# Cosine attention and a GELU feed-forward layer: the last 256 rows of w_in loaded in two column halves

## The chip, the core and the metric

The kernel runs on one core of one Trainium2 chip. The metric is the device time of one execution in microseconds (us), lower is better. The core has a matrix engine (TensorE, "PE" in the profile), a vector engine (VectorE, "DVE"), an activation engine (ScalarE, "ACT"), a general engine (GpSimd, "POOL") and a synchronising engine (SyncE, "SP") that issues most of the DMA transfers. "PEld" is TensorE's weight load, which runs beside its matmuls. SP, ACT and POOL issue DMA transfers; those of POOL can change the type on the way (here 32-bit floats in memory to bf16 on the chip).

## The reference

Eight batches of 12 heads of 448 rows by 64 go through attention with normalised queries and keys. The result, as 3584 rows of 768, goes through two matrix products with an exact GELU between them.

```python
q_n = q / (norm(q, axis=-1) + 1e-06)            # q, k, v: (8, 12, 448, 64)
k_n = k / (norm(k, axis=-1) + 1e-06)
scores = q_n @ k_n.T / tau                      # tau = 0.1
attn = exp(scores - max(scores))
attn = attn / (sum(attn) + 1e-09)
x = (attn @ v).transpose(0, 2, 1, 3).reshape(3584, 768)
h = x @ w_in                                    # w_in: (768, 2048)
g = 0.5 * h * (1 + erf(h / sqrt(2)))
out = g @ w_out                                 # w_out: (2048, 768)
```

## The kernel before

The order of the work is written out by hand; each engine runs its instructions in that order, and semaphores hold an instruction until what it needs is there.

Heads are worked on in groups of four (a "quad"): three groups to a batch, 24 in all, counted from 0. (The steps of `attention_first` are numbered by units: group 0 is units 0 and 1, group g is unit g + 1.) For a group, q and k are loaded by SP (`load_qk`, L122 to 132), squared (`square`, L156 on GpSimd), summed (`reduce`, L165 on VectorE), and turned into reciprocal norms: logarithm and exponential on ScalarE (`logs`, `roots`, L172, L178, L181), a small add on GpSimd (L190) and a reciprocal on VectorE (L192). `scale` (L208, GpSimd) multiplies by them and writes bf16. `transposes` turns the result, on TensorE with copies by VectorE (L225, L230) for the first four groups, and by a DMA transpose issued from SP (L220) afterwards. `scores` (L246) are matmuls, `exps` (L253) ScalarE; `sums` (L266, L275) and `values` (L289) are matmuls again, and `turned`, `inverted`, `spread` and `normalise` (L297 to L323, VectorE) make the finished columns of x.

The feed-forward layer runs batch by batch. `first(b)` (L647) forms h for one batch: sixteen blocks m of 128 columns of w_in, each the sum of six matmuls over the six row tiles kd of w_in (L659), followed by the GELU on ScalarE (L696). It takes row tiles 0 to 3 for the first blocks ("ahead", five for batch 0) and only then row tiles 4 and 5 for these blocks, since the last columns of x come last. At m = 8 of batch 0 TensorE also turns group 3. After m = 5 of batch 0 ScalarE computes the norms of groups 4 and 5. The second product (L352) is cut into single matmuls that are filled in between the attention work of the next batch. SP stores the results (L341).

`attention_first` (L407) writes out the order for batch 0 line by line. The weights are loaded there, between GpSimd's computing, by DMAs issued from GpSimd: `load_wi` (L381) brings 256 rows of w_in at a time, in two transfers (one for each of two sets of 128 rows, laid on 64 partitions each), so that load n holds row tiles 2n and 2n + 1, with all 2048 columns. Loads 0, 1 and 2 stand at L420, L453 and L493. `load_wo` (L387) brings a quarter of w_out, `load_v` (L137) the values. All of GpSimd's transfers are in one queue (q0 in the profile) and go in the order of issue; those of SP are in another (q1), and the same 16 DMA engines serve both. Every GpSimd transfer uses one of eight semaphores in turn, so the issue of one waits until the one eight places before it has landed. `upto(f, n)` (L396) calls the steps of `f` that are still to be done, up to n of them. `spin` (L402) is a matmul without use.

The step around the change is L493 to L524: third load of w_in, the scale of group 2 (q at L483, k at L499), then the squares of groups 3 and 4 (L514 to L525), a part of w_out (L526) and the values of batch 1 (L527).

Of the kernel before, what the change touches and what calls it, by code (L numbers as in the profile page):

```python
# [16 lines left out]
def kernel(  # L17
# [18 lines left out]
    B, H, S, D = q.shape  # L36
    C = S // D
    NQ = H // 4
    NG = B * NQ
    d_model = H * D  # L40
    d_ff = moe_w_in.shape[1]
# [49 lines left out]
    wi = wpool.tile([128, KD, d_ff], BF16, tag="wi")  # L91
# [21 lines left out]
    NU = len(units)  # L113
    groups = [[n] for n in range(NQ + 2)] + [[NQ + 2, NQ + 3], [2 * NQ + 1], [2 * NQ + 2]]
# [20 lines left out]
    NV = len(v_parts)  # L135
# [64 lines left out]
    def scale(u, parts=None):  # L200
        g, s0, s1 = units[u]
        n, j = place[u]
        rn = rn_t[n][:, j]
        if g not in qkb_t:
            qkb_t[g] = qkbp.tile([128, 2, C, 2, D], BF16, tag="qkb", name=f"qkb{g}")
        qkb, t = qkb_t[g], qk_t[g]
        for eng, i in parts or ((nc.gpsimd, 0), (nc.gpsimd, 1)):
            eng.tensor_tensor(  # L208
                qkb[:, i, :, s0:s1].rearrange("p c s d -> p s c d"), t[:, i, s0:s1],
                rn[:, i].to_broadcast([128, s1 - s0, C, D]), ALU.mult)  # L210
# [16 lines left out]
    def copies(u, i):  # L227
        g, s0, s1 = units[u]
        rows = slice(64 * s0, 64 * s1)
        nc.vector.tensor_copy(qkT_t[g][rows, i], tp_t.pop((u, i))[rows])  # L230
# [47 lines left out]
    def values(g, chunks=range(C), p=None):  # L278
        for c in chunks:
            if c == 0 and g < NQ:  # L280
                bank_t[g, 0] = ps_acc.tile([128, 512], F32, tag="o", name=f"o{g}_0")
                bank_t[g, 1] = mm_tile(f"o{g}_1")
            elif c == 0:
                o = pair(p, f"o{g}")
                bank_t[g, 0], bank_t[g, 1] = o[:, 0], o[:, 1]
            for s in range(2):
                for h in range(2):
                    rows, cols = slice(64 * h, 64 * (h + 1)), slice(64 * s, 64 * (s + 1))
                    nc.tensor.matmul(bank_t[g, h][cols, :S], lhsT=v_t[g][rows, s, c, :],  # L289
                                     rhs=pt_t[g, s, c][rows], start=(c == 0), stop=(c == C - 1),  # L290
                                     tile_position=(64 * h, 64 * s))
# [86 lines left out]
        return [lambda c0=c0, c1=c1: part(c0, c1) for c0, c1 in ((0, 3 * n), (3 * n, 5 * n), (5 * n, 6 * n))]  # L378


    def load_wi(n):  # L381
        for s in range(2):
            nc.gpsimd.dma_start(
                out=wi[64 * s:64 * (s + 1), 2 * n:2 * n + 2, :],
                in_=moe_w_in.rearrange("(n s h d) f -> n s d h f", s=2, h=2, d=D)[n, s])

    def load_wo(i):  # L387
        n, c = KF // 2, slice(i // 2 * NH, (i // 2 + 1) * NH)
# [5 lines left out]
    done = {}  # L394

    def upto(f, n, last=None):  # L396
        last = {load_qk: NG, load_v: NV, root: len(groups), load_wi: NQ, load_wo: 4}.get(f, NU)
        while done.get(f, 0) < min(n, last):
            done[f] = done.get(f, 0) + 1
            f(done[f] - 1)  # L400
# [6 lines left out]
    def attention_first():  # L407
# [6 lines left out]
        reduce(0, K)  # L414
        square(1, ((AC, Q),))
        upto(load_v, 1)
        logs(0)
        reduce(1, Q)
        roots(0)
        upto(load_wi, 1)  # L420
        square(1, ((AC, K),))
        inverses(0)
# [17 lines left out]
        square(3, ((AC, K),))  # L440
        scale(1, ((GP, 1),))
        upto(load_qk, 5)
        spin(1)
        transposes(1, 0)
# [6 lines left out]
        scores(0, ((0, 2), (0, 3)))  # L451
        roots(2)
        upto(load_wi, 2)  # L453
        exps(0, ((0, 0), (0, 1)))
        inverses(2)
# [35 lines left out]
        exps(1, ((0, 0), (1, 0)))  # L491
        sums(0, (6,))
        upto(load_wi, 3)  # L493
        transposes(3, 0)
        turned(0)
        exps(1, ((0, 1), (1, 1)))
        scores(1, ((0, 2), (1, 2)))
        values(0, (0,))
        scale(3, ((GP, 1),))  # L499
        copies(3, 0)  # L500
        values(0, (1,))
        exps(1, ((0, 2), (1, 2)))
# [221 lines left out]
    for b in range(B):  # L724
        if b == 0:
            attention_first()
            acc.close()
            third.append(ctx.enter_context(tc.tile_pool(name="ps_third", bufs=1, space=bass.MemoryType.PSUM)))
        else:
            attention(b, fill)  # L730
        first(b)
        sb, hf = divmod(b, 2)
        todo = [(t, ni) for t in (range(3) if hf == 0 else range(3, 7)) for ni in range(2)]
        if b == 0:
            todo.sort(key=lambda x: x[1])
        tail = [2 * S // 128 - 1] if b == B - 1 else []
        fill = [f for t, ni in todo if t not in tail for f in second_pieces(sb, t, ni)]
        fill += [f for t in tail for f in last_pieces(sb, t)]
# [37 lines left out]
```

## Time and profile before

| | |
|---|---|
| median of 4 runs | 416.23 us (415.62 to 416.30) |
| the profiled execution, its own time | 417.82 us |
| its span, first to last instruction | 416.0 us |
| TensorE busy | 407.1 us (98%) |
| ScalarE busy | 248.8 us (60%) |
| VectorE busy | 188.1 us (45%) |
| GpSimd busy | 166.4 us (40%) |
| granted TensorE clock, mean | 0.996 |
| DMA: w_in, six transfers of 512 KB | 15.9 us median from issue to landing |

Times inside the profile are counted from the start of the span. A row of a timeline gives the start, the length (of all instructions merged into the row), the engine, the line, the operation, what is written and read, how many instructions, and in brackets the idle time of the engine just before and what ended it. Where an instruction waits for several things, the bracket names the one that came last. A granted clock of 1.00 is full speed and 0.50 is half. A row of the slices gives tenths in 40 slices of 10.4 us. Sizes of GpSimd's transfers are those written on the chip.

### The profile page before, as it was taken

The page shows a single profiled execution, that of the slowest core. Times are in us where ns is not written, and L with a number is a line of the kernel's source. Part 1 is how long each engine was busy: PE and PEld are TensorE (multiplying, and loading weights), DVE is VectorE, ACT ScalarE, POOL GpSimd, SP SyncE. Part 2 cuts the span into 40 slices and gives each one's busy share as a digit, 9 for nine tenths or more (in the row PEclk, how much of TensorE's full clock was granted, in tenths as well). Part 3 has the DMA queues.
Part 4 walks back from the last instruction along what each step waited for, and adds up shares of the span by engine and source line. Part 5 has one row for each costly group of instructions (what it writes and reads, how often), then busy time and mean ns, then how long its engine had stood idle before and what let it go on. Part 6 is the DMA issues. An engine that isn't in the chain of part 4 may idle for free.

```text
span 416.0 us, 8265 instructions
## 1 busy us (share of the span) xinstructions
PE 407.1 (98%) x3503; PEld 212.1 (51%) x3503; DVE 188.1 (45%) x379; ACT 248.8 (60%) x362; POOL 166.4 (40%) x113
## 2 busy tenths in 40 slices
PE   7997999999999999999999999999999999999996
PEld 3443555555555555555555555555555555555564
DVE  5786203943167322853148431683118711481021
ACT  6993677657745657745764548755655467754300
POOL 5998625066730719045540446318270243000000
PEclk9998999999999999999999999999999999999999
DMA  8999996834297314946197242975079130610033
GB/s 286 259 256 215 205 237 211 202 74 130 46 198 242 70 66 59 229 162 134 23 183 241 47 125 46 185 220 132 2 134 225 38 46 0 121 39 2 0 77 76
DMA packets 66196, 54.53 MB, mean 131 GB/s; under 512 B 38640, under 2 KB 62320, under 8 KB 66160
## 3 DMA queue, kind: packets, MB, share of 16 engines
q1 hardware_dynamic: 54464, 41.79, 39.2%
q0 software_dynamic: 11312, 11.80, 17.8%
q8 instruction: 27, 0.44, 0.5%
q10 hardware_dynamic: 384, 0.43, 0.3%
q14 instruction: 9, 0.07, 0.1%
HBM read 45.61 MB, written 11.01 MB: 136 GB/s over the span
## 4 chain that ended last, share of the span: by engine, by line
PE 90%; DMA 6%; ACT 1%; SPq 1%; POOL 0%; issue 0%; DVE 0%; DVEq 0%
PE op L352 35%; PE hp L659 35%; PE st L246 8%; PE o L289 7%; DMA wi<-in_moe_w_in_dram 4%; PE sm L275 4%; DMA qk<-in_k_dram 2%; PE op L371 1%; ACT pt L253 1%; SPq L129 1%; POOL qkb L208 0%; ACT sq L154 0%; PE tp L225 0%; ACT lq L172 0%; ACT root L178 0%
## 5 line engine op out<-in xcount | busy, mean ns | idle before, releaser
L253 ACT ACTIVATE pt<-st 128x896 bf16<-128x896 f32 x168 | 142.6, 916 | 65.6 <-PE st L246 65.5
L659 PE MATMUL hp<-x,wi 128*128 128x448 bf16 x768 | 148.8, 355 | 2.3 <-DMA wi<-in_moe_w_in_dram 2.3
L352 PE MATMUL op<-wo,g 128*128 128x384 bf16 x864 | 147.8, 326 | 0.0
L352 PEld LDWEIGHTS <-g 128*128 128x128 bf16 x864 | 81.5, 98 | 62.1 <-issue 10.7
L659 PEld LDWEIGHTS <-wi 128*128 128x128 bf16 x768 | 74.9, 98 | 75.1 <-issue 7.7
L696 ACT ACTIVATE g<-hp 128x448 bf16<-128x448 f32 x128 | 65.6, 545 | 71.8 <-PE hp L659 71.5
L208 POOL TENSOR_TENSOR qkb<-qk,rn 128x896 bf16<-128x896 f32 (+1 forms) x50 | 80.2, 1630 | 40.3 <-DVE rn L192 40.2
L356 DVE COPY ot<-op 128x384 f32<-128x384 f32 x54 | 29.6, 548 | 101.1 <-PE op L352 99.1
L156 POOL TENSOR_TENSOR sq<-qk 128x1792 f32<-128x1792 f32 (+1 forms) x22 | 66.6, 3036 | 12.3 <-DMA qk<-in_k_dram 12.1
L165 DVE TENSOR_REDUCE nq<-sq 128x28 f32<-128x1792 f32 (+2 forms) x30 | 48.7, 1635 | 49.4 <-POOL sq L156 46.1
L190 POOL TENSOR_SCALAR se<-sr 128x28 f32<-128x28 f32 (+1 forms) x15 | 4.5, 303 | 129.2 <-ACT sr L181 118.7
L246 PE MATMUL st<-qkT 64*64 64x448 bf16 x672 | 47.8, 358 | 0.1
L289 PE MATMUL o<-pt,v 64*64 64x448 bf16 x672 | 37.3, 352 | 0.0
L246 PEld LDWEIGHTS <-qkT 64*64 64x64 bf16 x672 | 18.2, 105 | 23.0 <-issue 14.9
L192 DVE RECIPROCAL rn<-se 128x28 f32<-128x28 f32 (+2 forms) x19 | 6.9, 364 | 50.3 <-POOL se L190 50.1
L318 DVE STREAM_TRANSPOSE rs<-rc 128x448 f32<-128x448 f32 x48 | 28.1, 623 | 0.8
L323 DVE TENSOR_TENSOR x<-o,rs 128x448 bf16<-128x448 f32 x48 | 27.0, 598 | 0.4
L289 PEld LDWEIGHTS <-v 64*64 64x64 bf16 x672 | 17.7, 106 | 16.7 <-issue 8.1
L297 DVE STREAM_TRANSPOSE tr<-sm 128x448 f32<-128x448 f32 x24 | 15.5, 647 | 13.4 <-PE sm L275 11.1
L275 PE MATMUL sm<-pt,ones 128*32 128x448 bf16 (+1 forms) x336 | 17.8, 332 | 0.0
L309 DVE TENSOR_REDUCE tr<-tr 32x28 f32<-32x28 f32 x84 | 16.5, 196 | 1.6
L275 PEld LDWEIGHTS <-ones 128*32 128x32 bf16 x336 | 6.8, 96 | 9.0 <-issue 7.2
(42 smaller groups left out, 118.4 us busy)
## 6 DMA issues: line engine op xcount, KB each, us to landing
qk<-in_q_dram SPq DMA_DIRECT2D x23, 448.0 KB, 6.9
qk<-in_k_dram SPq DMA_DIRECT2D x23, 448.0 KB, 9.2
out_dram<-ot SPq DMA_DIRECT2D x48, 192.0 KB, 3.5
v<-in_v_dram POOLq DMA_DIRECT2D x7, 672.0 KB, 12.4
wi<-in_moe_w_in_dram POOLq DMA_DIRECT2D x6, 512.0 KB, 15.9
wo<-in_moe_w_out_dram POOLq DMA_DIRECT2D x4, 768.0 KB, 14.1
out_dram<-ot SPq DMA_DIRECT2D x12, 96.0 KB, 2.2
qk<-in_q_dram SPq DMA_DIRECT2D x2, 224.0 KB, 3.4
```

Source lines behind the costliest of these rows:

```text
L156: eng.tensor_tensor(sq[:, part], t[:, part], t[:, part], ALU.mult)
L165: nc.vector.tensor_reduce(nq[:, part], sq[:, part], mybir.AxisListType.X, ALU.add)
L208: eng.tensor_tensor(qkb[:, i, :, s0:s1].rearrange("p c s d -> p s c d"), t[:, i, s0:s1], rn[:, i].to_broadcast([128, s1 - s0, C, D]), ALU. ...
L246: nc.tensor.matmul(st[cols, n, :S], lhsT=qkT[rows, 1, c, cols], rhs=qkT[rows, 0, :, cols], start=True, stop=True, tile_position=(64 * s, 6 ...
L253: nc.scalar.activation(pt[:, :m], st[:, :m, :S], AF.Exp, scale=inv_tau)
L275: nc.tensor.matmul(bank_t[g, "sm"][r:r + 32, cols], lhsT=ones, rhs=pt_t[g, s, c][:, cols], start=(c < 2), stop=(c >= C - 2), tile_position ...
L289: nc.tensor.matmul(bank_t[g, h][cols, :S], lhsT=v_t[g][rows, s, c, :], rhs=pt_t[g, s, c][rows], start=(c == 0), stop=(c == C - 1), tile_po ...
L318: nc.vector.transpose(rs, bank_t[g, "rc"][:, h].to_broadcast([128, NB, 32]))
L352: nc.tensor.matmul(ps[:, :NH], lhsT=g_t[sb][:, kf, t * 128:(t + 1) * 128], rhs=wo[:, kf, ni * NH:(ni + 1) * NH], start=(kf == 0), stop=(kf ...
L356: nc.vector.tensor_copy(ot[:, ni * NH:(ni + 1) * NH], ps[:, :NH])
L659: nc.tensor.matmul(hps[m], lhsT=wi[:, kd, m * 128:(m + 1) * 128], rhs=x_t[b][:, kd, :], start=(kd == 0), stop=(kd == KD - 1))
L696: nc.scalar.activation(g_t[sb][:, m, hf * S:(hf + 1) * S], hps.pop(m), AF.Gelu)
```

## The change

The third load of w_in (rows 512 to 767) is made as two loads: columns 0 to 1023 at the place of the old one, columns 1024 to 2047 behind the second part of group 2's scale, ahead of the squares of group 3. Each is again two transfers, so GpSimd issues eight transfers of w_in instead of six.

```diff
-    def load_wi(n):
+
+    def load_wi(i):
+        n = min(i, NQ - 1)
+        half = d_ff // 2
+        cols = slice(0, d_ff) if n < NQ - 1 else slice((i - n) * half, (i - n + 1) * half)
         for s in range(2):
             nc.gpsimd.dma_start(
-                out=wi[64 * s:64 * (s + 1), 2 * n:2 * n + 2, :],
-                in_=moe_w_in.rearrange("(n s h d) f -> n s d h f", s=2, h=2, d=D)[n, s])
+                out=wi[64 * s:64 * (s + 1), 2 * n:2 * n + 2, cols],
+                in_=moe_w_in[:, cols].rearrange("(n s h d) f -> n s d h f", s=2, h=2, d=D)[n, s])
...
-        last = {load_qk: NG, load_v: NV, root: len(groups), load_wi: NQ, load_wo: 4}.get(f, NU)
+        last = {load_qk: NG, load_v: NV, root: len(groups), load_wi: NQ + 1, load_wo: 4}.get(f, NU)
...
         scale(3, ((GP, 1),))
+        upto(load_wi, 4)
         copies(3, 0)
```

## The prediction

> **What bounds the kernel now.** The page comes first. TensorE (PE) is busy 98% of the span, so a gain must come from the remaining 2% or from work that runs below full speed. The slice rows show where.
>
> ```profile
> span 416.0 us, 8265 instructions
> PE   7997999999999999999999999999999999999996
> PEclk9998999999999999999999999999999999999999
> DMA  8999996834297314946197242975079130610033
> ```
>
> The fourth slice (31.2 to 41.6 us) is the only one after the start where PE drops to 7 and its granted clock below 9; DMA is full there. The list of waits and PE's timeline name the hole.
>
> ```profile
> PE hp L659 <- DMA wi<-in_moe_w_in_dram: 2.3, 1, 2.3
> ```
> ```profile
> 31.75 3.96 PE L659 MATMUL hp<-x,wi 128*128 128x448 bf16 x20
> 37.98 7.14 PE L659 MATMUL hp<-x,wi 128*128 128x448 bf16 x28 [2.27 <-DMA wi<-in_moe_w_in_dram]
> 44.96 0.94 PE L225 MATMUL tp<-ident,qkb 128*128 128x128 bf16 x14
> ```
>
> Twenty matmuls (row tiles 0 to 3 of w_in, blocks m = 0 to 4) run to 35.71; the next needs rows 512 to 767 and starts at 37.98. The chain of waits carries this as one piece:
>
> ```profile
> 19.98 17.86 DMA wi<-in_moe_w_in_dram
> 37.98 7.14 PE hp L659 x28
> 45.12 0.78 PE tp L225 x14
> 45.90 9.08 PE hp L659 x48
> ```
>
> 28 matmuls take 7.14 us here and 48 take 9.08 us just behind: 255 against 189 ns. The table by stage tells why (the third number from the end is the granted clock):
>
> ```profile
> 35.57:38.99 3.42, 1.15 (x7) 0.58 (x7) 0.79 (x1) 0.06 (x1) 2.06 (x2) 1.00 1.29 204
> 38.99:42.40 3.41, 3.41 (x11) 1.40 (x10) 2.02 (x1) 2.33 (x5) 3.12 (x3) 0.50 1.31 204
> 42.40:45.81 3.41, 3.41 (x30) 2.12 (x28) 0.00 (x0) 2.85 (x5) 0.35 (x1) 1.00 1.28 207
> ```
>
> A stretch with PE 34% busy is followed by one at clock 0.50. The wait costs 2.27 us and, behind it, 7.14 - 28 x 0.1925 = 1.75 us (0.1925 is 9.24 us over 48, from the timeline's row at 45.74): 4.0 us together. From 45.7 us on PE has no idle piece over 0.15 us before the end.
>
> **The change, part by part.**
> *The first halves.* At the place of the old pair (issued 19.34 and 19.98, landed 35.03 and 37.84) two transfers bring columns 0 to 1023, enough for m = 0 to 7. The queue is in order; the pair before it landed at 31.49, so 6.35 us went to this pair. Price of a packet, from transfer counts: 768-byte packets alone (38 to 48 us, 2554 of them) 64 ns per engine; 4096-byte ones (32 to 35 us, 0.57 MB, after taking off 84 packets of the SP queue at 75 ns) 300 ns. A 2048-byte packet lies between these two; by length 155 ns. Sixteen per engine are 2.5 us, plus 123 SP-queue packets left (31.5 to 37.9 us), 7.7 per engine at 75 ns, 0.6 us. The same sum gives the old pair 36.9 and it landed at 37.84, so I add half to all of that 1.0: landing 35.0 to 35.5 (ends of the bounds: 33.1 at 64 ns, 37.84 at 300). PE asks at 35.71. I take the wait as gone.
>
> A rule against splitting, "DMA: Bandwidth & Descriptors" of the Trainium skill (section on the anatomy of a gpsimd DMA): about 2.0 us fixed per transfer plus bytes over 436 GB/s. By it a half saves only 0.6 us, the pair would land at 36.6 and leave 0.9 us of wait. The trace disagrees for queued transfers: at 35 us 768-byte packets of the next transfer already flow while the last 4096-byte ones finish, so the fixed part is not paid between them; I keep 35.0 to 35.5.
>
> *The second halves.* Two more GpSimd issues of 0.62 us behind the scale that ends at 22.31. In the built order each GpSimd DMA past the eighth waits for the one eight before it: the new ones for v and the first w_in transfer (landed 13.03 and 16.28), then w_out for 19.43 and 25.25, v for 28.46, w_out again for 31.49 and the first halves. All are over when asked, so no stall. They land after the first halves with the same bytes, about 38; m = 8 asks at 42.
>
> *What the 1.25 us push back on GpSimd.* The squares of group 3 end at 26.8 (VectorE reduces them at 28.87: hidden). The next square loses only 1.05 because it waited 0.19 for its data at 25.6. w_out and v issues, 1.05 later, land much ahead of their use. The small add L190 starts at 32.6 instead of 31.64 (ScalarE's input, at 31.55, had almost no slack), so the reciprocal L192 behind it starts at 33.1 instead of 32.10, and behind that on VectorE wait the spreads and the last x tiles, ready at 35.4 instead of 34.43.
>
> ```profile
> 31.64 0.28 POOL L190 TENSOR_SCALAR se<-sr 128x28 f32<-128x28 f32 x1
> ```
> ```profile
> 32.10 0.27 DVE L192 RECIPROCAL rn<-se 128x28 f32<-128x28 f32 x1
> 32.28 1.11 DVE L318 STREAM_TRANSPOSE rs<-rc 128x448 f32<-128x448 f32 x2
> 33.31 1.12 DVE L323 TENSOR_TENSOR x<-o,rs 128x448 bf16<-128x448 f32 x2
> 34.35 2.00 DVE L165 TENSOR_REDUCE nq<-sq 128x28 f32<-128x1792 f32 x1
> ```
>
> PE needs x at 35.71: hidden, but by 0.3 us only. Cost 0: with the whole 1.25 they are ready at 35.6 to 35.7, still in time. The other end is 0.5, if the two issues cost as much as those of w_out do (0.90 to 0.96 each).
>
> *Clock.* With no hole the 0.50 stretch should go: 1.75 more, by the rows above. "TensorE: Matmul & The Clock Gate" of the Trainium skill (section "What's actually happening") puts half clock behind a whole idle window of about 3.4 us; by that rule a 2.27 us hole costs no clock and the gain would be 2.27. Here 2.27 us within 3.42 sufficed, so the row decides.
>
> *What is late next.* (a) ScalarE, after m = 5, needs the norms of groups 4 and 5: square at 37.15 (waiting for k at 36.99), reduce to 42.4. Before, ScalarE asked at 44.74; now at about 40.7, so it waits to 42.1. The reciprocal and two copies follow on VectorE to 44.7; PE asks for the bank of m = 10 at 44.3, the first copy is done about 44.1. Cost 0 to 0.3. (b) The first DMA transpose is issued when two scales are done: 47.1 instead of 49.78. It landed at 58.65, behind w_out, on engines that are full from 38 to 53 us. The engines' total work is unchanged and full, so I leave its landing at 58.65 (not the 56.0 of a shift by 2.7). PE asked for it in the scores at 61.99, third group of four, 62.2; with 3.85 gained, at 58.35. Cost 0.3.
>
> ```profile
> 49.78 4.18 SPq L220 DMA_TRANSPOSE qkT<-qkb  x1
> 54.08 0.51 SPq L129 DMA_DIRECT2D qk<-in_q_dram  x1
> 54.63 0.47 SPq L129 DMA_DIRECT2D qk<-in_k_dram  x1
> 55.26 5.03 SPq L220 DMA_TRANSPOSE qkT<-qkb  x1
> ```
>
> After 63 us each piece hangs on PE and shifts with it (the second transpose lands at 62.66 and is used at 71, before; 67 after).
>
> **Sum.** 2.27 + 1.75 - 0.15 (a) - 0.3 (b) = 3.6 us. The profiled execution took 417.82 us (span 416.0 and 1.8 around it) and should become 414.2. It is 1.6 us above the median of 416.23. I carry the 3.6 over: 412.6, stated as 412.7.
>
> **Rivals.**
> *Half clock only in the profiled execution.* The 1.6 us between it and the median is close to 1.75. If the timed runs have the wait without the slow stretch, the gain is 2.27 less 0.1 to 0.6: 414.3 (413.7 to 415.2). For it: that coincidence. Against it: four runs within 0.7 us say nothing of the cause, and a hole of the same length should slow the clock alike.
> *The wait stays.* If a half-size packet costs near its 300 ns bound or the slowest engine sets the landing, PE still starts near 37.5 and the clock drops: 415.6 to 416.3. Against it: bytes explain both measured packet prices.
> *The transpose becomes the wait, and the run slower.* Issued into w_out's stream, it may alternate packet by packet with it, as the SP and GpSimd queues do at 24 to 32 us (361 against 367 packets). With the later transpose's 5.03 us to issue it starts at 52.1; w_out then has some 44 packets per engine left (268 per us until 54, 191 after) and the transpose 112 (1792 in all); 44 pairs at 78 + 38 ns (mean times of a packet at 49 to 53 and 54 to 58 us) and 68 at 38 ns end at 59.8, landing 60.5, later on the slowest engine. PE would idle from 58.35, over 2 us, and the clock halve again (1.75). From a landing at 60.5 this eats all 3.85; at 61.5 the time is 417.3. Against it: total work before that landing does not grow.
>
> **How the numbers follow.** Forecast 0.50 (412.7; own range 411.9 to 413.6), clock rival 0.28, the wait stays 0.12, transpose 0.10. The range 411.9 to 415.3 leaves out the last two and a few per cent. 0.2% (0.83 us) is about what a measurement of this kernel tells from no change: faster than 415.4 in the first two and a part of the third, 0.81; same 0.10; slower 0.09.
>
> **What would show it.** Right: the row of 28 matmuls starts at 35.7 with no wait on w_in and takes about 5.4 us; no stretch at 0.50 in the clock; the two new issues at 22.3 without idle time; the add L190 at 32.6; m = 8's matmuls without a wait. (a) shows as ScalarE waiting for VectorE near 42; (b) as PE waiting on the transpose near 58. Wrong: first halves landing after 36, PE waiting for x at 35.7, a new half-clock stretch near 58, or a gain that is there at 55 us and gone by 65.

## The result and the profile after

The changed kernel takes 414.77 us in the median of 48 executions (lowest 414.04), the kernel before 416.22 us in 72 (lowest 415.15). The medians are 1.45 us apart. The ratio of the means, the slowest executions left out, is 0.9957, with a 95% interval of 0.9944 to 0.9970: 1.8 us (1.2 to 2.3), which leaves in four executions of the kernel before at 420.6 to 421.0 us and leaves out five of the changed kernel's six above 420. At full clock the means are 1.2 us apart (worked out below). The change makes the kernel faster, by a third to a half of the 3.6 us that were forecast; the time lies inside the stated range (411.9 to 415.3) and outside the likeliest case's own (411.9 to 413.6). (In two profiles, one of the changed kernel with 419.64 us and one of the unchanged with 421.28, TensorE ran at half clock from 13.3 us to 23.5 and 26.9; "at full clock" below means executions with a mean granted clock of 0.998 or more.) The median is nearest to the first rival, "half clock only in the profiled execution", at 414.3.

The page of the changed kernel, its head and three slice rows:

```profile
span 413.0 us, 8268 instructions
PE   7999999999999999999999999999999999999996
PEclk9999999999999999999999999999999999999999
DMA  8999999652495506944396332965088130610033
```

The dent in the fourth slice is gone from PE and from its clock. The profiled execution took 414.78 us, as the median does; that of before had taken 417.82, 1.6 us over its median. PE's timeline, same columns as before:

```profile
32.17 9.25 PE L664 MATMUL hp<-x,wi 128*128 128x448 bf16 x48
41.26 0.94 PE L225 MATMUL tp<-ident,qkb 128*128 128x128 bf16 x14
42.04 9.38 PE L664 MATMUL hp<-x,wi 128*128 128x448 bf16 x48
...
58.44 0.38 PE L246 MATMUL st<-qkT 64*64 64x448 bf16 x4
59.13 0.57 PE L246 MATMUL st<-qkT 64*64 64x448 bf16 x8 [0.31 <-DMA qkT<-qkb]
```

The 20 and the 28 matmuls of w_in have become one row of 48 without idle time, at the full rate (9.25 us, as the 9.24 of the later row before). The group of twelve score matmuls, which was one row at 61.99, is cut in two: four run, then PE waits for the first DMA transpose. The rows of the engines that lead there:

```profile
22.67 1.25 POOL L387 DMA_DIRECT2D wi<-in_moe_w_in_dram  x2
...
33.05 0.28 POOL L190 TENSOR_SCALAR se<-sr 128x28 f32<-128x28 f32 x1
```
```profile
34.64 1.11 DVE L323 TENSOR_TENSOR x<-o,rs 128x448 bf16<-128x448 f32 x2
```
```profile
42.33 0.34 ACT L172 ACTIVATE lq<-nq,tiny 128x56 f32<-128x56 f32 x1 [1.29 <-DVE nq L165]
```
```profile
47.37 5.06 SPq L220 DMA_TRANSPOSE qkT<-qkb  x1
```

The two new issues take 1.25 us and wait for nothing. The small add L190 starts 1.4 us later than before (0.4 of it because this execution was already that late ahead of the change: GpSimd's first issue of the third load is at 19.78, not 19.34, and PE's row begins at 32.17, not 31.75). The last x tiles are ready at 35.75; PE, which began at 32.17, asks for them after twenty matmuls, at 36.05. The transpose is issued at 47.37 and, by the trace, lands 11.7 us later, at 59.09. From the first score matmul of that group to the row behind it PE now needs 1.19 us (58.44 to 59.63); before it was 0.70 (61.99 to 62.69). So the wait costs 0.5 us in this execution.

### The profile page after: what moved, and what is told of

Same layout as the page of the kernel before. It is cut to its first block, busy times and chain, and to the rows that moved or that the text cites. A ratio compares the mean times of both kernels' runs of the same rounds, so it can differ in the third digit from the quotient of the medians.

```text
span 413.0 us, 8268 instructions
## 1 busy us (share of the span) xinstructions
PE 406.8 (98%) x3503; PEld 212.2 (51%) x3503; DVE 188.4 (46%) x379; ACT 248.4 (60%) x362; POOL 167.5 (41%) x115
## 4 chain that ended last, share of the span: by engine, by line
PE 87%; POOL 5%; DMA 3%; DVE 2%; ACT 1%; issue 1%; DVEq 0%
PE op L352 34%; PE hp L664 31%; PE st L246 8%; PE o L289 7%; PE sm L275 4%; DMA qkT<-qkb 3%; POOL qkb L208 2%; PE spin L409 2%; POOL sq L156 2%; PE op L371 1%; ACT pt L253 1%; DVE nq L165 1%; POOL wi L387 1%; POOL wo L394 0%; DVE rn L192 0%
## 5 line engine op out<-in xcount | busy, mean ns | idle before, releaser
L664 PE MATMUL hp<-x,wi 128*128 128x448 bf16 x768 | 147.1, 353 | 0.0
L190 POOL TENSOR_SCALAR se<-sr 128x28 f32<-128x28 f32 (+1 forms) x15 | 4.5, 303 | 123.8 <-ACT sr L181 123.7
L409 PE MATMUL spin<-blank,ident 128*128 128x448 bf16 x31 | 9.9, 458 | 2.0 <-DVE root L89 1.9
```

What stands on the lines that cost most here:

```text
L664: nc.tensor.matmul(hps[m], lhsT=wi[:, kd, m * 128:(m + 1) * 128], rhs=x_t[b][:, kd, :], start=(kd == 0), stop=(kd == KD - 1))
```

## The experiments

A clock given for an execution is its mean granted TensorE clock; a time "at full clock" is the median of such executions.

**The unchanged kernel once more, for its clock.** No edit.

> The unchanged kernel once more, to see clock and time of many executions. Theory (the wait on w_in is always there, the half-clock stretch behind it only in some executions): the times fall into groups by mean granted clock, most near 1.000 at 415.2 to 416.7 us, some near 0.996 (one stretch of 3.41 us at half) about 1.75 us longer, 417.5 to 418.2. Rival (the stretch is in every execution and the profile merely adds time): all executions near 0.996, in one group.

Of the twelve executions six ran at full clock, 415.37 to 416.60 us. One at 0.996 took 418.41. The 29 executions of the kernel before beside it, the same: 22 at full clock (median 416.06), one at 0.996 (419.50). In all executions of the unchanged kernel whose clock was listed (93, these and later ones), 71 were at full clock, three at 0.996 and one at 0.994. So the rival is out: the half-clock stretch of the forecast's profile is an exception. The theory holds in kind; of the three at 0.996 one is where it was expected (418.06) and two are later (418.41 and 419.50), and where they lost their time was not recorded. How rare such an execution is stays open: in the first measurement, which lists no clocks for the kernel before, 13 of its 72 times lie between 417.1 and 419.6 us, and none of the 48 of the changed kernel. And the wait itself was shorter in this profile:

```profile
32.40 3.96 PE L659 MATMUL hp<-x,wi 128*128 128x448 bf16 x20
37.29 5.46 PE L659 MATMUL hp<-x,wi 128*128 128x448 bf16 x28 [0.93 <-DMA wi<-in_moe_w_in_dram]
```

PE came 0.65 us later (its twenty matmuls began at 32.40, not 31.75), w_in landed 0.69 us earlier (37.15, not 37.84): 0.93 us of wait in place of 2.27, and the 28 matmuls take 5.46 us in place of 7.14.

**Two more profiles of the unchanged kernel.** No edit.

> One more profile of the unchanged kernel. Theory (the profile that the forecast was made from had an unusually long wait): PE waits 0.9 to 1.6 us on w_in at about 36.2, no stretch at half clock behind it, own time 415.4 to 416.5. Rival: 2.2 us and half clock again.

PE waited 1.38 us (35.88 to 37.26), with no half clock behind it, and the execution took 415.42 us.

> As the look before it, to see how far the wait on w_in varies from one execution to the next: 0.9 to 2.3 us, and a half-clock stretch only with the long ones.

This one took 421.28 us for another reason: half clock from 13.28 to 26.93 us, so that PE came to w_in at 43, long after the landing at 37.00, and did not wait for it at all. It says nothing of how long the wait is otherwise; it shows that w_in's landing does not move with PE.

**Both halves at the old place.** The split without the move.

```diff
-        upto(load_wi, 3)
+        upto(load_wi, 4)
...
-        upto(load_wi, 4)
```

> Both column halves issued at the old place, nothing moved. Theory (the split alone removes the wait): first halves land at 35.0 to 35.5 as in the changed kernel, no wait of PE on w_in, no half clock. The two extra issues (1.25 us) now stand ahead of the k half of group 2's scale, where PE's transposes have 0.4 us to spare, so 0.3 to 0.8 us of the gain may go: 414.8 to 415.6. Rival (the place matters): the gain is gone, 416.

415.43 us at full clock (eleven executions). The first halves landed at 33.88 and 35.00, PE did not wait for w_in. The extra issues, now ahead of the k half of group 2's scale, cost PE a wait of their own:

```profile
24.18 0.56 PE L225 MATMUL tp<-ident,qkb 128*128 128x128 bf16 x7 [0.71 <-POOL qkb L208]
```

So the split takes the wait away, and in this profile the place of the second issue costs 0.7 us. In the times it is less clear: at full clock they are 0.75 us over the changed kernel's in the median, but 0.44 in the mean (standard error 0.17), and four of the eleven, 414.38 to 414.65 us, are as fast as the changed kernel. How often this wait is paid stays open.

**The move without the split.**

```diff
-        upto(load_wi, 3)
...
         scale(3, ((GP, 1),))
+        upto(load_wi, 3)
```

> The whole third load of w_in issued behind group 2's scale, not split. Theory: its queue holds older transfers until 31.3, so an issue 1.7 us later lands at the same 35.0 and 37.8, PE waits 2.2 us again: 416 us, same as before. Rival (the place of the issue sets the landing): landing and PE 1.7 us later, 417.5 or more with more half clock.

415.94 us at full clock (eight executions), as before. Issued at 21.30 and 21.94 the two transfers landed at 34.44 and 37.35, no later than with the issue at 19.34 and 19.98; PE waited 1.48 us. Within these 2 us the landing is set by what stands ahead in the queue, not by the moment of issue.

**Only the wait taken away.** Loads and orders of the kernel before; batch 0 takes other rows of w_in, which are there already.

```diff
-                nc.tensor.matmul(hps[m], lhsT=wi[:, kd, m * 128:(m + 1) * 128],
+                nc.tensor.matmul(hps[m], lhsT=wi[:, kd - 2 if b == 0 and kd >= KD - 2 else kd, m * 128:(m + 1) * 128],
```

> The kernel before, in which batch 0 multiplies with row tiles 2 and 3 of w_in in place of 4 and 5 (that part of the result is another number); loads and orders are untouched, PE need not wait for the third load. Theory (the wait on w_in was the whole gain, the extra issues cost nothing): as the changed kernel, 414.4 to 414.9, with PE waiting on the transpose near 58.5. Rival (the two extra issues and the later x cost something): 0.3 us or more faster than the changed kernel. Other rival (part of the gain came from the moved issues): slower than the changed kernel by 0.3 or more.

414.62 us at full clock (eleven executions), with PE waiting 0.35 us for the transpose at 58.45. The changed kernel is at 414.57 (ten executions beside it) and 414.68 (42 of the first measurement); the means are 414.66 and, over these 52, 414.72. So at full clock the wait on w_in is the whole gain; the two extra issues and the later x cost nothing that these runs can show. The twelfth execution took 417.91 us at a mean clock of 0.991, so a time of this kind does not need the wait on w_in.

For the ten beside it the changed kernel was run once more; 414.5 to 414.9 us at full clock were expected, and a wait of 0.2 to 0.6 us for the transpose. The time came out so. The profile does not show the wait: it took an execution of 419.64 us, with half clock from 13.26 to 23.50, in which PE came to that group at 63.83, long after the landing at 59.96.

**The split at three quarters.**

```diff
-        half = d_ff // 2
-        cols = slice(0, d_ff) if n < NQ - 1 else slice((i - n) * half, (i - n + 1) * half)
+        cut = 3 * d_ff // 4
+        cols = slice(0, d_ff) if n < NQ - 1 else (slice(0, cut), slice(cut, d_ff))[i - n]
```

> The split at column 1536 instead of 1024. Theory (landing goes by bytes: 16 packets per engine took 3.9 us after 31.3, so 24 packets take about 5.1): first part lands at 36.2 to 36.6, PE waits 0.1 to 0.6 us for it, and the wait on the transpose near 59 shrinks by as much, since its landing does not move: 414.6 to 415.0, as the half split. Rival (a wait on w_in adds to the time in full): 0.1 to 0.6 us longer than the half split.

414.49 us at full clock (nine executions), as the half split. The first part landed at 36.39, in the expected place. In the profile PE waited for neither it nor the transpose, because it had lost 0.9 us to a wait for the values at 25.5 and asked at 36.8. The time fits the theory; the profile did not show the trade of one wait for the other.

**w_out's last part issued later.** The changed kernel, with:

```diff
-            upto(load_wo, 4)
...
         if b == 1:
+            upto(load_wo, 4)
             upto(load_qk, g0 + NQ + 2)
```

> The changed kernel with the last two quarters of w_out issued behind the scales of groups 4 and 5 (about 50.7 instead of 40.2). Theory (w_out's packets hold up the first DMA transpose): the transpose lands at 51 to 54 instead of 59.1 and PE's wait near 58.8 goes (0.3 to 0.5 us); the last quarter of w_out, asked for at about 63.7, lands at 62 to 66, so a new wait of up to 2 us may take its place. Rival (the transpose is slow by itself): it lands at 57 or later all the same.

The first transpose was issued at 47.27 as ever, took 1.63 us to issue instead of 5.06, and landed at 51.33 instead of 59.09. This is SP's timeline:

```profile
47.27 1.63 SPq L220 DMA_TRANSPOSE qkT<-qkb  x1
```

w_out's traffic is what holds it up. But the price is far over the expected 2 us:

```profile
64.38 1.47 PE L352 MATMUL op<-wo,g 128*128 128x384 bf16 x8 [1.54 <-DMA wo<-in_moe_w_out_dram]
72.38 2.08 PE L352 MATMUL op<-wo,g 128*128 128x384 bf16 x6 [6.53 <-DMA wo<-in_moe_w_out_dram]
```

The last quarter landed at 72.3, not at 62 to 66 (it now shared the engines with the second transpose and four loads of q and k), and the clock was at half for 6.8 us behind the longer wait. The six executions took 421.5 to 433.0 us, none of them at full clock, 426.0 in the median. w_out is better early and in the transpose's way.

**Other work ahead of the transpose's user.** The changed kernel, with four matmuls of the second product in front of the third group of scores:

```diff
-            parts = iter((20, 13, 14, 17, 16, 16) if b == 1 else (16, 14, 16, 18, 16, 16))
+            parts = iter((20, 17, 10, 17, 16, 16) if b == 1 else (16, 14, 16, 18, 16, 16))
```

> The changed kernel with four matmuls of the second product (4 x 0.17 us) moved from behind the third group of scores of batch 1 to ahead of it (20, 17, 10 instead of 20, 13, 14). Theory (the transpose's landing near 59 is the last thing that PE waits for): the wait is covered, the time falls by 0.3 to 0.5 us, to 414.2 to 414.4. Rival (another wait stands right behind, on ScalarE's exponentials): no change, 414.6 to 414.8.

> The changed kernel with the four matmuls moved, again, since the first time showed it 0.3 us faster on few executions. Theory: 414.1 to 414.4 at full clock. Rival (chance): 414.6 to 414.7, as the changed kernel.

In both profiles the wait is gone (PE's timeline of the first):

```profile
56.07 2.94 PE L352 MATMUL op<-wo,g 128*128 128x384 bf16 x17
58.94 0.76 PE L246 MATMUL st<-qkT 64*64 64x448 bf16 x12
```

The times at full clock: 414.27 (eight executions), then 414.69 (twelve). Together a mean of 414.54, with a standard error of 0.11, against 414.72 with 0.05 for 52 executions of the changed kernel. The difference of 0.2 us is within two standard errors of nothing; whether covering the wait pays stays open, and 0.5 us is more than these times allow.

> The unchanged kernel with the four matmuls moved ahead of the third group of scores (20, 17, 10). Theory (in the unchanged kernel PE comes to that group after the transpose has landed, so there is nothing to cover): same, 415.8 to 416.2 at full clock. Rival (the order is better by itself): 0.3 us or more faster.

The same edit on the unchanged kernel gave 416.20 us at full clock (ten executions): no gain there either, as expected. Its profile happened to show a long wait at full clock, which settles the question of the clock.

## The clock behind the wait

The kernel before, with the fill edit, waited as long as the forecast's profile did (2.21 us against 2.27), yet ran on at full speed: 28 matmuls in 5.46 us, not 7.14. PE's timeline and the table by stage, cut at the multiples of 3.41 us at which the granted clock changes in the trace:

```profile
31.72 3.96 PE L659 MATMUL hp<-x,wi 128*128 128x448 bf16 x20
37.89 5.46 PE L659 MATMUL hp<-x,wi 128*128 128x448 bf16 x28 [2.21 <-DMA wi<-in_moe_w_in_dram]
```
```profile
33.08:36.50 3.42, 2.60 (x14) 1.15 (x12) 3.42 (x6) 0.00 (x0) 3.33 (x2) 1.00 1.12 211
36.50:39.91 3.41, 2.02 (x11) 1.10 (x12) 0.57 (x1) 1.06 (x3) 1.94 (x1) 1.00 1.30 204
39.91:43.32 3.41, 3.41 (x22) 1.80 (x20) 2.02 (x1) 3.12 (x6) 3.03 (x3) 1.00 1.31 205
```

Here the wait is split over two stretches, with PE busy 2.60 and 2.02 us of each; in the forecast's profile it fell into one, busy 1.15 us. The edges lie at other places in each execution (counted from the span's start, the first at 4.86 in the forecast's profile, at 5.78 in this one). Half clock behind a stretch that is only partly idle shows also in the profile of the changed kernel that took 419.64 us, in its first microseconds:

```profile
9.85:13.26 3.41, 1.72 (x19) 0.86 (x17) 3.34 (x7) 2.06 (x4) 1.99 (x3) 1.00 1.16 290
13.26:16.67 3.41, 2.97 (x17) 1.33 (x17) 1.59 (x4) 2.50 (x5) 2.23 (x4) 0.50 1.07 242
16.67:20.09 3.42, 3.42 (x15) 0.63 (x12) 2.23 (x3) 2.33 (x3) 2.90 (x2) 0.50 1.06 254
20.09:23.50 3.41, 3.41 (x26) 1.76 (x24) 1.10 (x3) 2.44 (x5) 1.21 (x1) 0.50 1.18 271
```

Here a stretch with PE busy 1.72 of 3.41 us (50%) is followed by half clock; above, one with 2.02 (59%) is not. But PE's busy time alone does not decide it, as the late w_out shows, around its wait of 6.53 us:

```profile
63.95:67.36 3.41, 1.47 (x8) 0.80 (x9) 0.00 (x0) 0.21 (x1) 0.00 (x0) 1.00 1.16 274
67.36:70.77 3.41, 0.00 (x0) 0.00 (x0) 0.00 (x0) 0.00 (x0) 1.23 (x1) 1.00 1.12 307
70.77:74.18 3.41, 1.80 (x6) 0.84 (x6) 0.00 (x0) 0.00 (x0) 2.77 (x2) 0.50 0.40 129
```

Behind the stretch with 1.47 us busy (43%) the clock stayed full, and only behind the empty one it was at half. Nor does one busy stretch always end half clock: it did behind the forecast's wait, but in the execution of 419.64 us PE was busy all through 16.67 to 20.09 and the next stretch was still at half. These stretches hold different matmuls (all of 128 by 128 in the forecast's profile and with the late w_out, many of 128 by 64 and 64 by 64 in the other one at 10 to 20 us); whether that counts was not tested, so what exactly decides the clock stays open.

The two executions with the long wait took 417.82 and 416.07 us (own times; the latter's span of 414.3 and 1.8 around it): 1.75 us apart, as the forecast had it for the slow stretch.

The Trainium skill, "TensorE: Matmul & The Clock Gate" (section "What's actually happening"), says that the window is free-running and does not start with the kernel; the moving edges agree. It also puts half clock behind a whole idle window. With the late w_out it took one; in the forecast's profile a window with PE busy for 34% of it was enough.

## Why the prediction was right or wrong

*The first halves and the wait.* Right. Expected at 35.0 to 35.5, they landed at 33.51 and 35.17; the second halves, expected about 38, at 36.39 and 37.62. The wait on w_in is gone. Landings 1.2 to 1.7 us apart also bear out that queued transfers do not each pay a fixed part of 2 us. By the fit in "DMA: Bandwidth & Descriptors" of the Trainium skill (section on the anatomy of a gpsimd DMA) a transfer of 256 KB would take an estimated 2.6 us. (A slip in the prices: the packets between 38 and 48 us were not all of 768 bytes, since the values of batch 1, with 896, landed at 48.68; 2554 packets in 10 us are 63 ns, not 64. The landing hardly feels it.)

*The second halves' issues.* Right: 1.25 us, no stall on the older transfers. x ready at 35.75 with PE asking at 36.05 is the 0.3 us of margin that the forecast named, and leaving out the wait alone gives the same time as the change.

*The sum's first two terms.* Here the prediction failed. "2.27 + 1.75" was read off one execution and carried over to the median. The 1.75 of half clock is not in most executions: four of 93 show a mean clock of 0.994 to 0.996, and a wait of the same length was followed by full clock where it spanned an edge. (A part is in the average all the same: executions under 420 us in the first measurement have means of 416.41 and 414.75, 1.7 us apart and not 1.2, because of the 13 between 417.1 and 419.6; whether these lost their time behind w_in was not recorded.) And 2.27 was the longest of the waits seen: 0.93, 1.38 and 2.21 in profiles of the same loads at full clock, 1.48 with the load moved. The wait is the difference of two moments that vary by themselves, PE's arrival (35.7 to 36.4) and the landing (37.1 to 37.8). The profiled execution's 1.6 us over the median was the sign, and the first rival said so; it was given 0.28 and the forecast 0.50, although the only number at hand, these 1.6 us, spoke for the rival. The stated range held the measured time because it took in that rival. The rival's own sum has the long wait's 2.27 us, too; that it comes within 0.5 us of the median is in part luck.

*What is late next, (a).* Right: ScalarE waits 1.29 us for the norms, until 42.33 (forecast 42.1), and the eight blocks from m = 8 on take 9.38 us instead of 9.24, 0.14 us against 0.15.

*(b), the transpose.* Right in place and kind, a little short in size: it landed at 59.09 (forecast 58.65) and cost 0.5 us, not 0.3. The late w_out shows the cause: with w_out out of the way it landed at 51.33. The forecast's picture of an earlier issue came from the one profile, too: the unchanged kernel at full clock issued the transpose at 47.38 and 47.51, hardly later than the changed one (47.37), and it landed at 58.32 and 58.25, 0.8 us earlier; why the changed kernel's landed later is not shown. The landing is a floor for everything behind it: in the changed kernel the scores that need it cannot start before about 59.1, where the unchanged kernel started them at 59.9 (59.62 and four matmuls in the second profile) or, in the forecast's, at 62.2.

*The sum in the right sizes.* At full clock the means are 415.94 (71 executions, standard error 0.05) and 414.72 (52, 0.05): 1.2 us. The three waits seen in the unchanged loads at full clock have a mean of 1.5; less 0.14 for (a), and less 0.5 or nothing for (b), this gives 0.9 to 1.4. How the 1.2 is made up in the timed executions, whose waits were not recorded, stays open.

*The other rivals.* The wait did not stay. The transpose became the next wait but not at the price of the slower rival (from 60.5 on); its landing moved by 0.4 us against the forecast's profile. That the engines' total work fixes it was argued and not shown.

## What to carry to other kernels

A stall read from one profile is one draw: where it is the gap between two streams that vary by themselves, look at more executions before multiplying it out, and take a profiled time well above the median as a warning that the profile shows a loss the others don't have. When a load is late because its queue is full, issuing it at another moment may do nothing (here 2 us later did not); asking for fewer bytes first does, and the second part should be issued where its engine has time to spare. Before booking the whole stall, look for the next transfer that does not move with it: here the transpose's landing, held up by w_out's traffic, took back 0.5 us in the profiled execution.

## What the runs showed of the hardware

The granted clock changed at multiples of 3.41 us, with edges that differ between executions. Stretches with TensorE busy for 34% and 50% were followed by half clock and one with 59% was not, but neither was one with 43%, so busy time alone gives no threshold here. The same 2.2 us of idle time was followed by half clock, at a cost of 1.75 us, in one execution and by full clock in another. A DMA transpose issued while another queue's 768-byte packets fill the engines took 5.06 us to issue and landed after 11.7 us; with only the last of the values in that queue it took 1.63 and 4.1 us.
